# A spectral and token-mixing kernel: the order of PE and DVE written out, statistics block by block, products of a zeroed tile, moved tables and gate sums

## The chip, the core and the metric

The kernel runs on one core of a Trainium2 chip. A core has a matrix engine (PE) that multiplies a 128x128 stationary operand into a moving one and accumulates in PSUM, a vector engine (DVE), an activation engine (ACT), a general engine (POOL), and a queue engine (SP) that here only starts DMAs. Each runs its own list of instructions in order and waits on semaphores for the others. The metric is the device time of one execution in microseconds, lower is better; the runs before the change have a median of 156.61 us.

## What is computed

x is 2048 rows of 512, in bf16. The result mixes two branches, row by row, with a gate.

```python
g = _sigmoid((x * gate_w).sum(-1, keepdims=True))
# a: spectral filter
X = jnp.fft.rfft2(x.astype(jnp.float32), axes=(-2, -1)) * (w_r + 1j * w_i)
a = jnp.fft.irfft2(X, s=(S, D), axes=(-2, -1)).astype(jnp.bfloat16)
# b: token-mixing MLP, over the 2048 rows
h = _layernorm(x)
u = _gelu(jnp.einsum("bsd,sf->bdf", h, w1) + b1)
b = (jnp.einsum("bdf,fs->bds", u, w2) + b2).transpose(0, 2, 1)
return g * a + (1 - g) * b
```

S is 2048, D is 512, and the hidden width F is 1792, that is 14 columns of 128.

## The kernel before

**The MLP branch** works on x in 16 blocks of 128 rows. For each block, DVE makes mean and variance (`moments`: bn_stats, bn_aggr, an addition; POOL then takes the power -1/2), and DVE or ACT writes the normalised block hn (`normal`). The first six hidden columns (FT1 = 6) are accumulated over all 16 blocks at once in six PSUM banks, u1, from the weights w1a: six products of 128x512 per block (L248). The other eight columns come later, 16 products each, from w1b (L492). ACT evicts each column through a gelu into gl (`gelu`, L334). Then every block of the output takes 14 products from w2t into a bank yb (L505), which ACT evicts into tbv with the factor omg = 1 - g and the bias ombb2 (L507).

**The spectral branch** is a two-dimensional FFT by factors. xt is x transposed by four DMAs; the folds (L328, L329) make xf, sums and differences of its halves. Step f1 multiplies xf with the table tf into xdt, 16 blocks of four 256-column products (L343), each copied out by ACT (L345). `fft16` does a 16-point FFT across blocks on DVE alone, in two stages (p, r, q, s and their combinations), into fu. Step f3 multiplies fu with the table tce, 16 times three products (L414 to L417), and ACT copies to xs. `weight` multiplies four xs at a time with the filter wri into y (L407 to L410); a small side path (wn, ws, wrev, ghc with the permutations pmA and pmB, products L379 and L381, then u0, q, gu) treats the lowest column. Step i1 goes back with tice (L462, L464) into vp, a second `fft16` gives zt, step ya multiplies with tg (L478), ACT scales it by the gate (eo), DVE adds the halves (ap), and ot = tbv + ap is stored.

**The tables** tf, tg, tce and tice are sines: DVE makes integer arguments (m1t, m4t, marg, marg3), masks them to a period, and ACT takes the sine. Sines and gelus need different ACT tables, hence the ACT_TABLE_LOAD instructions. **The gate** is prod = x * gate weights on DVE (L323), summed per block by ACT with an accumulator (L352) into glog.

**What sets the order.** Between `startup.__enter__()` and `startup.__exit__()` the order of DVE, ACT, POOL and SP is that of the code, except that PE is not in the list. A planner orders PE everywhere and all engines after the exit; it puts products of u2 and yb into PE's free places. SP starts x and w1a in four pairs, then two transposes, w1b[0], two transposes, the rest of w1b, and wri. [...] PSUM has six banks for u1, u2 and yb and two ("ab") for f1, f3, i1, ya and the small steps. Scratch tiles with one tag share one buffer: `ffr` holds marg3 and then r of the FFT.

```python
startup = tc.manual_schedule(engines={E.DVE, E.Activation, E.Pool, E.SP})
home = {"x": 0, "fa": 0, "xs": 0, "ia": 0, "hn": 1, "vp": 1, "zt": 1, "xt": 2, "xdt": 2, "fu": 2, "ap": 2,
        "marg": 5, "xf": 3, "ea": 6, "y": 3, "wri": 4, "gl": 5, "prod": 6, "tbv": 6}
marg3 = tmp.tile([P, 2, NE, P], I16, tag="ffr", name="marg3")
```

`home` names the memory plane of each large tile; tiles in one plane follow each other in time.

Of the kernel before, what the change touches and what calls it, by code (L numbers as in the profile page):

```python
# [23 lines left out]
FT1 = 6  # L24
PI_IN = 3.1415925
# [80 lines left out]
def kernel(  # L106
# [24 lines left out]
    home = {"x": 0, "fa": 0, "xs": 0, "ia": 0, "hn": 1, "vp": 1, "zt": 1, "xt": 2, "xdt": 2, "fu": 2, "ap": 2,  # L131
            "marg": 5, "xf": 3, "ea": 6, "y": 3, "wri": 4, "gl": 5, "prod": 6, "tbv": 6}
# [11 lines left out]
    startup = tc.manual_schedule(engines={E.DVE, E.Activation, E.Pool, E.SP})  # L144
    startup.__enter__()

# [4 lines left out]
    for b0, b1 in ((0, 2), (2, 6), (6, 11), (11, 16)):  # L151
        w = wts.tile([P, b1 - b0, FT1 * P], BF16, tag="wt", name="w1a")
        nc.sync.dma_start(out=x[:, b0:b1], in_=xv[:, b0:b1])  # L153
# [4 lines left out]
    nc.gpsimd.dma_start(out=bias_rows[0:NFT], in_=B_b1.rearrange("(ft f) -> ft f", f=P))
    nc.gpsimd.dma_start(out=bias_rows[NFT:NFT + NB], in_=B_b2.rearrange("(b a) -> b a", a=P))
# [55 lines left out]
    nc.vector.tensor_copy(m1[:, :, 0], fix[:])  # L215
# [11 lines left out]
    def moments(b0, b1):  # L227
        bs = slice(b0, b1)
        for b in range(b0, b1):
            nc.vector.bn_stats(out=stats[:, b, :], in_=x[:, b, :])  # L230
        for b in range(b0, b1):
            nc.vector.bn_aggr(out=mv[:, b, :], in_=stats[:, b, :])
        nc.vector.tensor_scalar_add(rstd[:, bs], mv[:, bs, 1], 1e-5)
        nc.gpsimd.tensor_tensor(rstd[:, bs], rstd[:, bs], c_mhalf.to_broadcast([P, b1 - b0]), op=Alu.pow)
# [308 lines left out]
```

## Time and profile before

| | |
|---|---|
| runs | 156.5, 156.59, 156.63, 157.9 us; median 156.61 |
| profiled execution | 156.5 us, of which the span on the core is 154.7 us |
| granted PE clock, mean | 0.993 |
| instructions | 2013 |
| HBM | 19.02 MB read, 2.10 MB written |

The span runs from the first to the last instruction that the profiler recorded; the rest of an execution's time lies around it. In the timelines, a row has the start in us, the length, engine, line of the code, operation, the tile written and those read with partitions x elements and type, and the number of instructions merged; brackets hold the engine's idle time ahead of it and what ended that. In the groups, busy time and the mean in ns of one instruction stand behind the count. Lengths of neighbours overlap, so one instruction of a row of n costs a little less than its length.

### The profile page before, as it was taken

The numbers are of one execution on the slowest core, as the hardware profiler recorded it, in microseconds if no ns is written. First come the engines' busy times: TensorE is split into PE (matmuls) and PEld (weight loads), VectorE is DVE, ScalarE is ACT, GpSimd is POOL, SyncE is SP. The second block draws the span as 40 slices with busy tenths as digits, with TensorE's granted clock in tenths as the row PEclk, the third lists the DMA queues.
The fourth block names the chain that finished last, engine by engine and source line by source line (L and its number), as shares of the span: only waits on it lengthen the run. The fifth ranks groups of instructions, "written<-read, shape, count | busy, mean of one in ns | idle before, by whom it ended". The sixth has DMA issues, their size and how long they took to land.

```text
span 154.7 us, 2013 instructions
## 1 busy us (share of the span) xinstructions
PE 135.6 (88%) x697; PEld 68.0 (44%) x697; DVE 116.6 (75%) x279; ACT 94.7 (61%) x150; POOL 12.8 (8%) x37
## 2 busy tenths in 40 slices
PE   0078999969899999999959999999999969989990
PEld 0023444424456544444335565465444435655430
DVE  3988979969900399999994999507999999888111
ACT  3305564997199999999628897457223224978221
POOL 7117725000000000000000000000000000000000
PEclk9999999999999999999999999999999999999997
DMA  5999999999999304361800800250166100334210
GB/s 155 273 376 395 257 194 306 261 278 269 322 306 308 113 0 118 119 202 35 236 2 0 238 6 0 69 168 4 46 192 197 41 0 0 135 108 143 91 36 34
DMA packets 41816, 23.33 MB, mean 151 GB/s; under 512 B 9008, under 2 KB 41776, under 8 KB 41808
## 3 DMA queue, kind: packets, MB, share of 16 engines
q1 hardware_dynamic: 41696, 23.08, 52.6%
q0 software_dynamic: 112, 0.14, 0.3%
q8 instruction: 5, 0.08, 0.2%
q14 instruction: 3, 0.02, 0.1%
HBM read 19.02 MB, written 2.10 MB: 137 GB/s over the span
## 4 chain that ended last, share of the span: by engine, by line
DVE 46%; PE 21%; SPq 17%; ACT 7%; DMA 6%; issue 2%; DVEq 0%; ACTq 0%
SPq L172 10%; PE yb L505 9%; PE f L343 5%; DMA xt<-in_A_x_dram 4%; SPq L153 3%; DVE ta L407 3%; DVE prod L323 3%; DVE tb L408 3%; SPq L154 3%; ACT tice L204 2%; DMA out_dram<-ot 2%; DVE y L409 2%; PE ya L478 2%; DVE pb L39 2%; DVE ra L40 1%
## 5 line engine op out<-in xcount | busy, mean ns | idle before, releaser
L505 PE MATMUL yb<-gl,w2t 128*128 128x512 bf16 x224 | 53.6, 379 | 0.0
L505 PEld LDWEIGHTS <-w2t 128*128 128x128 bf16 x224 | 21.9, 98 | 21.5 <-issue 0.2
L492 PE MATMUL u<-hn,w1b 128*128 128x512 bf16 x128 | 29.3, 379 | 1.2 <-ACT gl L334 1.2
L507 ACT ACTIVATE tbv<-yb,ombb,omg 128x512 bf16<-128x512 f32 x16 | 12.4, 778 | 23.8 <-PE yb L505 22.4
L248 PE MATMUL u<-hn,w1a 128*128 128x512 bf16 x96 | 24.3, 419 | 1.5 <-DVE hn L245 1.5
L492 PEld LDWEIGHTS <-w1b 128*128 128x128 bf16 x128 | 12.5, 98 | 15.1 <-issue 1.5
L248 PEld LDWEIGHTS <-w1a 128*128 128x128 bf16 x96 | 10.1, 106 | 15.3 <-issue 6.1
L242 ACT ACTIVATE hn<-x,nmr,rstd 128x512 bf16<-128x512 bf16 x13 | 9.6, 802 | 9.8 <-DVE nmr L239 7.6
L481 ACT ACTIVATE eo<-ya,gs 128x512 bf16<-128x512 f32 x16 | 10.4, 687 | 4.9 <-DVE ap L484 2.7
L345 ACT CAST xdt<-f 128x512 bf16<-128x512 f32 x16 | 10.6, 735 | 4.0 <-DVE xf L329 3.5
L511 DVE TENSOR_TENSOR ot<-tbv,ap 128x512 bf16<-128x512 bf16 x16 | 6.7, 421 | 8.1 <-ACT tbv L507 7.5
L418 ACT CAST xs<-f 128x512 bf16<-128x512 f32 x16 | 9.1, 588 | 4.1 <-PE f L417 3.8
L478 PE MATMUL ya<-tg,zt 128*128 128x256 bf16 x64 | 9.3, 272 | 1.9 <-DVE zt L98 1.2
L466 ACT CAST vp<-i 128x512 bf16<-128x512 f32 x16 | 8.8, 587 | 2.8 <-PE i L464 2.6
L230 DVE BATCH_NORM_STATS2 stats<-x 128x6 f32<-128x512 bf16 x16 | 10.1, 680 | 0.4 <-DMA x<-in_A_x_dram 0.4
L352 ACT ACTIVATE junk<-prod 128x512 bf16<-128x512 bf16 x16 | 10.0, 626 | 0.3
L343 PE MATMUL f<-tf,xf 128*128 128x256 bf16 x64 | 9.6, 271 | 0.7 <-DVE xf L328 0.6
L334 ACT ACTIVATE gl<-u,biases 128x512 bf16<-128x512 f32 x14 | 9.0, 686 | 0.8 <-PE u L492 0.8
L478 PEld LDWEIGHTS <-zt 128*128 128x128 bf16 x64 | 6.1, 97 | 5.9 <-issue 1.9
L343 PEld LDWEIGHTS <-xf 128*128 128x128 bf16 x64 | 6.0, 96 | 5.5 <-issue 3.2
L462 PE MATMUL i<-tice,y 128*128 128x256 bf16 x32 | 7.8, 272 | 0.1
L39 DVE TENSOR_TENSOR pa<-xdt 128x2048 bf16<-128x2048 bf16 x1 | 1.2, 1225 | 8.9 <-ACT xdt L345 8.9
(178 smaller groups left out, 182.8 us busy)
## 6 DMA issues: line engine op xcount, KB each, us to landing
w2t<-in_B_w_dram SPq DMA_DIRECT2D x8, 896.0 KB, 5.1
w1b<-in_B_w_dram SPq DMA_DIRECT2D x4, 1024.0 KB, 8.9
out_dram<-ot SPq DMA_DIRECT2D x16, 128.0 KB, 1.7
w1a<-in_B_w_dram SPq DMA_DIRECT2D x2, 960.0 KB, 10.9
x<-in_A_x_dram SPq DMA_DIRECT2D x2, 640.0 KB, 10.6
wri<-in_A_w_r_dram SPq DMA_DIRECT2D x1, 1028.0 KB, 9.6
wri<-in_A_w_i_dram SPq DMA_DIRECT2D x1, 1028.0 KB, 10.1
w1a<-in_B_w_dram SPq DMA_DIRECT2D x1, 768.0 KB, 8.0
```

The lines of the kernel that those rows point to most:

```text
L172: nc.sync.dma_start(out=xt[:, dt], in_=xr[:, dt], transpose=True)
L230: nc.vector.bn_stats(out=stats[:, b, :], in_=x[:, b, :])
L242: nc.scalar.activation(hn[:, b, :], x[:, b, :], ActF.Identity, bias=nmr[:, b:b + 1], scale=rstd[:, b:b + 1])
L248: nc.tensor.matmul(u1[ft][:], lhsT=w1a[b][:, ft * P:(ft + 1) * P], rhs=hn[:, b, :], start=(b == 0), stop=(b == NB - 1))
L343: nc.tensor.matmul(bank[:, par * L:(par + 1) * L], lhsT=xf[:, par, kt, b * P:(b + 1) * P], rhs=tf[:, kt, par], start=(kt == 0), stop=(kt = ...
L345: nc.scalar.copy(xdt[:, b].rearrange("p c (i t) -> p t c i", t=2), bank[:].rearrange("p (t c i) -> p t c i", t=2, c=2))
L352: nc.scalar.activation(junk[:], prod[:, b], ActF.Copy, accum_out=glog[:, b:b + 1])
L478: nc.tensor.matmul(bank[:, par * L:(par + 1) * L], lhsT=zt[:, b, comp, par, :], rhs=tg[:, par, comp, :], start=(comp == 0), stop=(comp == 1))
L481: nc.scalar.activation(eo[:], bank[:].rearrange("p (t d) -> p t d", t=2), ActF.Copy, scale=gs[:, b:b + 1])
L492: nc.tensor.matmul(u[:], lhsT=w[:, b, k * P:(k + 1) * P], rhs=hn[:, b, :], start=(b == 0), stop=(b == NB - 1))
L505: nc.tensor.matmul(yb[:], lhsT=w[:, ft, k * P:(k + 1) * P], rhs=gl[:, ft, :], start=(ft == 0), stop=(ft == NFT - 1))
L507: nc.scalar.activation(tbv[:, b, :], yb[:], ActF.Identity, bias=ombb2[:, b:b + 1], scale=omg[:, b:b + 1])
```

## The change

It writes the order of PE too, up to the forward FFT, and that of DVE up to the last ap, and regroups the work:

- **Zero products.** PE starts with 12 products of a zeroed tile, into a bank that nobody reads.
- **Loads.** x and w1a come in eleven DMAs instead of eight, the first of a single block. On POOL, dcol and lrow come ahead of the two bias DMAs. The product that transposes the biases moves from PE's first place to behind block 9.
- **Statistics** go block by block, three stages interleaved (bn_stats of b, the rest of b-1, normalisation of b-2).
- **Gate.** Blocks 6 to 15 are multiplied and summed by one DVE instruction each; for 0 to 5 DVE multiplies in place and ACT sums. prod goes.
- **Folds** are done per pair of transposes, `fold(0)` and `fold(1)`, with six of the gate sums between.
- **Tables.** Arguments of tf and tg are 16-bit. tg, tce and tice are made behind the folds on DVE and behind f1 on ACT; marg, marg3 and ea share the plane idx, and fa lies in plane 3. The load of the gelu table is drawn ahead by a dummy gelu, `pre`.
- **PE order.** u1, hidden columns 6 and 7, f1 with column 8 threaded through it, columns 9 to 13, and the products of output blocks 0 and 1 (`yb_early`); from f3 on the planner fills in the other yb products.
- **Behind the FFT.** The sign and scale fixes of the tables, omg, gs, ombb2 and wn, ws follow the whole FFT on DVE; the rest of the side path (`packed_weights`) stands behind the second `weight`.

```diff
-    startup = tc.manual_schedule(engines={E.DVE, E.Activation, E.Pool, E.SP})
+    startup = tc.manual_schedule(engines={E.DVE, E.Activation, E.Pool, E.SP, E.PE})
+    zero = tmp.tile([P, D], BF16, tag="tws", name="zero")
+    nc.vector.memset(zero[:], 0.0)
+    warm = a_bank("warm")
+    for _ in range(WARM):
+        nc.tensor.matmul(warm[:], lhsT=zero[:, 0:P], rhs=zero[:], start=True, stop=True)
...
-    for b0, b1 in ((0, 2), (2, 6), (6, 11), (11, 16)):
-        w = wts.tile([P, b1 - b0, FT1 * P], BF16, tag="wt", name="w1a")
-        nc.sync.dma_start(out=x[:, b0:b1], in_=xv[:, b0:b1])
-        nc.sync.dma_start(out=w[:], in_=w1v[:, b0:b1, 0:FT1 * P])
...
+    for kind, b0, b1 in (("x", 0, 1), ("x", 1, 4), ("w", 0, 2), ("x", 4, 6), ("w", 2, 4), ("x", 6, 8), ("w", 4, 6), ("x", 8, 12), ("w", 6, 11), ("x", 12, 16), ("w", 11, 16)):
+        if kind == "x":
+            nc.sync.dma_start(out=x[:, b0:b1], in_=xv[:, b0:b1])
+        else:
+            w, g0 = wgroup[b0]
+            nc.sync.dma_start(out=w[:, b0 - g0:b1 - g0], in_=w1v[:, b0:b1, 0:FT1 * P])
...
-    m1t = tmp.tile([P, 2, 2, 2 * P], I32, tag="ffp", name="m1t")
+    m1t = tmp.tile([P, 2, 2, 2 * P], U16, tag="ffp", name="m1t")
...
+    def moments(b):
+        nc.vector.bn_aggr(out=mv[:, b, :], in_=stats[:, b, :])
+        nc.vector.tensor_scalar_add(rstd[:, b:b + 1], mv[:, b, 1:2], 1e-5)
+        nc.gpsimd.tensor_tensor(rstd[:, b:b + 1], rstd[:, b:b + 1], c_mhalf, op=Alu.pow)
...
+    sums(0)
+    moments(0)
+    for b in range(1, NB + 2):
+        if b < NB:
+            sums(b)
+        if b <= 3:
+            moments(b)
+            normal(b - 1)
+        elif b == 4:
+            normal_act(3)
+        elif b == 5:
+            moments(4)
+        else:
+            if b - 1 < NB:
+                moments(b - 1)
+            normal_act(b - 2)
...
+    pre = small.tile([P, 1], F32, name="pre")
+    nc.scalar.activation(pre[:], c_mhalf, ActF.Gelu_apprx_tanh)
+
+    def gate_sum(b0, b1):
         for b in range(b0, b1):
+            nc.vector.scalar_tensor_tensor(x[:, b], x[:, b], 1.0, gwb[:], op0=Alu.mult, op1=Alu.mult,
+                                           accum_out=glog[:, b:b + 1])
...
+    def fold(k):
+        nc.vector.tensor_add(xf[:, 0, k], xt[:, k], xt[:, k + 2])
+        nc.vector.tensor_sub(xf[:, 1, k], xt[:, k], xt[:, k + 2])
+
+    gate_sum(6, 10)
+    for b0 in (0, 3):
+        nc.vector.tensor_mul(x[:, b0:b0 + 3], x[:, b0:b0 + 3], gwb[:, None, :].to_broadcast([P, 3, D]))
+    fold(0)
...
+    gate_sum(10, NB)
+    fold(1)
...
+    for ft in (FT1, FT1 + 1):
+        u = mm_bank("u2")
+        for b in range(NB):
+            hidden(ft, u, b)
+        gelu(ft, u)
+    u = mm_bank("u2")
+    for b in range(NB):
...
+        if b >= 6:
+            hidden(FT1 + 2, u, b - 6)
+    for b in range(NB - 6, NB):
+        hidden(FT1 + 2, u, b)
+    gelu(FT1 + 2, u)
...
+    for ft in range(FT1 + 3, NFT):
+        u = mm_bank("u2")
+        for b in range(NB):
+            hidden(ft, u, b)
+        gelu(ft, u)
...
+    yb_early = [mm_bank("yb"), mm_bank("yb")]
+    for k in range(2):
+        for ft in range(NFT):
+            nc.tensor.matmul(yb_early[k][:], lhsT=early[:, ft, k * P:(k + 1) * P], rhs=gl[:, ft, :],
+                             start=(ft == 0), stop=(ft == NFT - 1))
...
+    nc.vector.tensor_scalar_mul(tce[:, 2], tce[:, 0], -1.0)
+    nc.vector.tensor_scalar_mul(tg[0:1, 0, :, :], tg[0:1, 0, :, :], 0.5)
+    nc.vector.tensor_scalar_mul(tice[:, :, 2], tice[:, :, 0], -1.0)
...
+    ombb2 = small.tile([P, NB], F32, name="ombb2")
+    nc.vector.tensor_mul(ombb2[:], omg[:], b2f)
...
+        if e == 7:
+            packed_weights()
...
+    def evict(b, yb):
+        nc.scalar.activation(tbv[:, b, :], yb[:], ActF.Identity, bias=ombb2[:, b:b + 1],
+                             scale=omg[:, b:b + 1])
+
+    for b in range(2):
+        evict(b, yb_early[b])
+    for c2 in range(1, NB // 2):
```

`normal(b)` and `normal_act(b)` do what `normal` did for one block on DVE or ACT and issue the block's six products; `sums(b)` is its bn_stats; `hidden(ft, u, b)` is one product of a later hidden column; `early` is w2t's first 256 columns.

The order of DVE around the start of the forward FFT. Before (L39 to L42 are p, q, r, s of the first stage, L54 to L59 parts of its output):

```order
L39 TENSOR_TENSOR pa<-xdt 128x2048
L41 TENSOR_TENSOR qa<-xdt 128x2048
L42 TENSOR_TENSOR sa<-xdt 128x2048
L54 TENSOR_TENSOR fa<-pa,qa 128x2048
L55 TENSOR_TENSOR fa<-pa,qa 128x1024
L56 TENSOR_TENSOR fa<-pa,qa 128x512
L58 TENSOR_TENSOR fa<-pa,qa 128x256
L59 TENSOR_TENSOR fa<-qa,pa 128x256
L349 TENSOR_SCALAR tice<-tice 128x16x128
L40 TENSOR_TENSOR ra<-xdt 128x2048
```

The same place after the change (idx holds the arguments of tce and tice):

```order
L380 TENSOR_TENSOR idx<-idx,m_374 128x2048
L381 TENSOR_SCALAR idx<-idx 128x2048
L215 TENSOR_SCALAR idx<-idx 128x4096
L391 TENSOR_SCALAR pmB<-spj 128x128
L392 TENSOR_SCALAR pmA<-spj 128x128
L393 TENSOR_SCALAR pmA_610<-spj 128x128
L394 TENSOR_TENSOR pmA<-pmA,pmA_610 128x128
L41 TENSOR_TENSOR pa<-xdt 128x2048
L42 TENSOR_TENSOR ra<-xdt 128x2048
L43 TENSOR_TENSOR qa<-xdt 128x2048
```

The table arguments and permutations have moved to right ahead of pa, and ra has moved from behind the tice fix to second place.

The order of ACT where the f3 copies (xs) begin. Before (junk, glog are the gate sums, tbv the eviction of an output block):

```order
L334 ACTIVATE gl<-u_1166,biases 128x512
L352 ACTIVATE junk,glog<-prod 128x512 x5
L334 ACTIVATE gl<-u_1184,biases 128x512
L354 ACTIVATE g<-glog 128x16
L507 ACTIVATE tbv<-yb,ombb_530,omg 128x512
L418 CAST xs<-f_626 128x512
L418 CAST xs<-f_631 128x512
```

After:

```order
L218 ACTIVATE tice<-idx,consts 128x2x16x128
L330 ACT_TABLE_LOAD
L330 ACTIVATE gl<-u_615,biases 128x512
L330 ACTIVATE gl<-u_633,biases 128x512
L330 ACTIVATE gl<-u_651,biases 128x512
L330 ACTIVATE gl<-u_669,biases 128x512
L330 ACTIVATE gl<-u_687,biases 128x512
L547 ACTIVATE tbv<-yb,ombb_810,omg 128x512 x2
L473 CAST xs<-f_820 128x512
L473 CAST xs<-f_825 128x512
```

The gate sums are gone from this place, the tice sine and its two table changes stand ahead of five gelus, and two evictions instead of one stand ahead of xs. Rows of the changed kernel carry its own line numbers.

260 lines of the change are left out of this document (114 added, 146 removed).

## The prediction

> **What bounds the kernel now.** I read the page's engine totals and its chain first, then busy time by stretch, then each engine's timeline at the stage borders.
>
> ```profile
> PE 135.6 (88%) x697; PEld 68.0 (44%) x697; DVE 116.6 (75%) x279; ACT 94.7 (61%) x150; POOL 12.8 (8%) x37
> DVE 46%; PE 21%; SPq 17%; ACT 7%; DMA 6%; issue 2%; DVEq 0%; ACTq 0%
> 12.00:16.20 4.20, 4.19 (x11) 1.45 (x11) 3.74 (x14) 2.22 (x3) 3.22 (x11) 1.00 1.07 394
> 16.20:33.60 17.40, 17.40 (x81) 7.82 (x80) 14.90 (x46) 13.03 (x14) 5.25 (x12) 1.00 1.12 249
> ```
>
> PE is the busiest engine, but the chain that ended last is nearly half DVE. In the stretches (length, then busy us and starts of PE, PEld, DVE, ACT and POOL, granted clock, DMA share, GB/s) 11 products start in 4.20 us, one per 0.4; after 16.2 it is one per 0.215, though the clock column reads 1.00 in both. I use 0.2155 us for a 512-column product (below: 40 in 8.80, the last of which lasts 0.38).
>
> ```profile
> 5.08 0.69 DVE L230 BATCH_NORM_STATS2 stats<-x 128x6 f32<-128x512 bf16 x1
> 26.01 0.18 DVE L302 COPY biases<-bias_t 128x30 f32<-128x30 f32 x1
> ...
> 33.39 4.63 DVE L323 TENSOR_TENSOR prod<-x,gwb 128x2048 bf16<-128x2048 bf16 x4
> 41.34 1.22 DVE L329 TENSOR_TENSOR xf<-xt 128x2048 bf16<-128x2048 bf16 x1
> 51.43 1.23 DVE L39 TENSOR_TENSOR pa<-xdt 128x2048 bf16<-128x2048 bf16 x1 [8.87 <-ACT xdt L345]
> 59.90 1.22 DVE L40 TENSOR_TENSOR ra<-xdt 128x2048 bf16<-128x2048 bf16 x1
> 78.78 1.22 DVE L100 TENSOR_TENSOR fu<-pb,qb 128x2048 bf16<-128x2048 bf16 x1
> 83.26 1.23 DVE L407 TENSOR_TENSOR ta<-xs,wri 128x2048 bf16<-128x2048 bf16 x1 [2.03 <-ACT xs L418]
> 98.24 0.68 DVE L410 TENSOR_TENSOR y<-tb,ta 128x1024 bf16<-128x1024 bf16 x1
> 105.56 1.23 DVE L39 TENSOR_TENSOR pa<-vp 128x2048 bf16<-128x2048 bf16 x1 [4.37 <-ACT vp L466]
> 129.06 1.22 DVE L100 TENSOR_TENSOR zt<-pb,qb 128x2048 bf16<-128x2048 bf16 x1
> ```
>
> This is DVE's timeline (start, length, work; in brackets the idle time ahead and its releaser). DVE does the statistics, the tables, prod and the folds until 42.6, idles 8.87 us, and runs the forward FFT from 51.4 to 80.0, 28.6 us. The inverse FFT, with nothing between, takes 105.56 to 130.3, 24.7 us.
>
> ```profile
> 42.64 2.75 ACT L345 CAST xdt<-f 128x512 bf16<-128x512 f32 x4 [3.50 <-DVE xf L329]
> 45.81 8.42 ACT L345 CAST xdt<-f 128x512 bf16<-128x512 f32 x12
> 55.54 3.71 ACT L204 ACTIVATE tice<-marg,consts 128x4096 bf16<-128x4096 int16 x1
> 59.68 0.19 ACT L352 ACTIVATION_READ_ACCUMULATOR junk<-prod 128x1 f32 x1
> 76.84 0.78 ACT L507 ACTIVATE tbv<-yb,ombb,omg 128x512 bf16<-128x512 f32 x1 [1.39 <-DVE ombb L360]
> 82.64 1.86 ACT L418 CAST xs<-f 128x512 bf16<-128x512 f32 x3 [0.19 <-PE f L417]
> ```
>
> On ACT the copies out of f1 wait for the folds and then run at 0.70 each (12 in 8.42). In the FFT ra comes only at 59.9: it takes the buffer of marg3, which the tice sine reads until 59.25.
>
> ```profile
> 24.81 8.80 PE L248 MATMUL u<-hn,w1a 128*128 128x512 bf16 x40
> 106.01 19.59 PE L505 MATMUL yb<-gl,w2t 128*128 128x512 bf16 x90
> 126.79 1.05 PE L478 MATMUL ya<-tg,zt 128*128 128x256 bf16 x8 [1.19 <-DVE zt L98]
> 140.84 9.66 PE L505 MATMUL yb<-gl,w2t 128*128 128x512 bf16 x44
> ```
>
> PE has spare yb products until 125.6, waits 1.19 us for the inverse FFT, and has 44 left when ya is done. So DVE's chain and PE's work meet within 1.2 us at 126.8, and a gain must shorten both.
>
> **The change, part by part.** The sum follows DVE; PE is checked beside it.
>
> *Start: loads, warm products, 16-bit tables.*
>
> ```profile
> 1.26 0.67 POOL L158 DMA_DIRECT2D bias_rows<-in_B_b_dram  x1 [0.81 <-POOLq L527]
> 2.55 0.16 POOL L183 IOTA dcol<- 128x2 f32 x1
> 4.47 0.69 DVE L201 TENSOR_SCALAR m1t<-m1t 128x1024 int32<-128x1024 int32 x1
> 1.76 0.46 SPq L153 DMA_DIRECT2D x<-in_A_x_dram  x1
> w1a<-in_B_w_dram SPq DMA_DIRECT2D x1, 384.0 KB, 3.2
> x<-in_A_x_dram SPq DMA_DIRECT2D x1, 512.0 KB, 6.5
> w1b<-in_B_w_dram SPq DMA_DIRECT2D x4, 1024.0 KB, 8.9
> ```
>
> dcol, on which the tables wait, moves ahead of POOL's two bias DMAs, 2.55 to 1.26. The mask of 1024 int32 takes 0.69, as long as 2048 int16 (below), so about 0.2 goes there: first statistics at 5.08 - 1.5 = 3.6. hn[0] then has the statistics of block 1 ahead of it, 2.3 in all: 5.9. w1a[0:2] is third in SP's queue, issued at 1.76: it lands between 5.0 (384 KB took 3.2 as the second) and 8.3 (the third took 6.5). I take 6.5, the middle, as PE's first product. The twelve warm products are through by then (from 1.3, at the cold pace of 0.42, until 6.4). They and the finer loads pull PE forward: 96 products from 6.5 end at 27.2 and two hidden columns (6.9) at 34.1. w1b[0] goes out ahead of the third transpose at 21.58 (below); at 8.9 it would land by 30.5, which moves 34.1 to 37.4 at worst. PE stands at 33.6 now when u1 ends, but what it gains counts only if DVE has the folds ready.
>
> *Statistics block by block.*
>
> ```profile
> L230 DVE BATCH_NORM_STATS2 stats<-x 128x6 f32<-128x512 bf16 x16 | 10.1, 680 | 0.4 <-DMA x<-in_A_x_dram 0.4
> 6.25 0.59 POOL L234 TENSOR_TENSOR rstd<-rstd,consts 128x1 f32<-128x1 f32 x1 [2.35 <-DVE rstd L233]
> ```
>
> Per block DVE needs 0.63 (10.1/16) and three small dependent instructions, together 0.4: 1.0 us. Bounds are 0.8 (the small ones packed) and 1.3 (a wait for a POOL power of 0.59 in each round). Blocks 1 to 3 add a normalisation, about 0.36. With 16 rounds, those, and 1.3 for the last two rounds and the bias copy, DVE is through at 3.6 + 16.0 + 1.1 + 1.3 = 22.0, against 26.2 now; bounds 18.8 and 26.8. PE's 6 x 0.2155 = 1.29 per block hides this pace. What left DVE here (tg, marg and marg3 tables) comes back behind the folds.
>
> *Gate sums and folds.* No row shows a two-source DVE instruction with an accumulator. Below it stands a quarter of a prod instruction, 0.3 (prod: 1.16 each); above, a statistics instruction (also 512 wide) plus ACT's accumulator read, 0.68 + 0.19 = 0.87. I take 0.75, nearer the row that also reduces; ten cost 7.5 (3.0 to 8.7). [...] Two products of 1536 take 1.75, four folds 4.55 (1.14 each), m0 and ae 0.55: fold 1 ends at 22.0 + 14.35 = 36.4. It also needs the last transpose, which the chain of waits shows:
>
> ```profile
> 21.58 5.26 SPq L172
> 26.88 6.04 DMA xt<-in_A_x_dram
> ```
>
> It landed at 32.9, behind the same bytes as after the change; with fold 1 behind it that gives 35.2. So DVE sets 36.4, PE (34.1) waits 2 us, and ACT, with six gelus, six sums of 0.75 and two gelus from about 26.5, is there at 36. The warm products and the loads are worth nothing past this point, unless DVE is faster than I think.
>
> *f1 and the tables.* With four products of 256 columns ahead (0.6) the first copy starts at 37.0; 16 at 0.70 end at 48.2, and the twelfth, which pa and ra need, at 45.4. The tables for tg, tce and tice now stand between fold 1 and pa on DVE (the DVE rows shown with the change).
>
> ```profile
> 17.13 1.39 DVE L258 TENSOR_SCALAR marg<-m,ae 128x128 int16<-128x128 int16 x8
> 26.20 0.69 DVE L307 TENSOR_SCALAR marg<-marg 128x2048 int16<-128x2048 int16 x1
> 30.05 1.23 DVE L201 TENSOR_SCALAR marg<-marg 128x4096 int16<-128x4096 int16 x1
> ```
>
> They cost 2 x 1.39, 5.1 for the five instructions from 26.20 to 31.28, about 1.5 for m4t in 16 bits and 0.8 for pmA and pmB: 10.2, so pa starts at 46.6. The former idle time pays for all but 1.2 us of it; if f1 came earlier this cover would be gone and the tables would hold pa. The sines lie on ACT behind the copies, and marg3 has a buffer of its own, so ra follows pa: 24.7 for the FFT gives 71.3, against 80.0.
>
> *Behind the FFT.* DVE then writes the three table fixes, omg, gs and ombb2 (1.8 by the widths above): 73.1. ACT has two evictions ahead of xs (the ACT rows with the change), which need ombb2 and take 2 x 0.73: 74.6. Four xs copies at 0.6 follow: the first weighting starts at 77.0, against 83.26. PE arrives with the early products at 72.2 (f1 and column 8 about 49, five columns 17.2, 28 products 6.0) and waits here too. The weighting stage took 98.92 - 83.26 = 15.7; packed_weights, now inside it, adds 1.3: 94.0. The inverse FFT starts 6.6 later and ya 21.2 after that: 121.8. PE beside it: its spare run starts 0.45 behind the FFT's start, at 101.1, and 91 products take 19.6: 120.7. DVE is late by 1.1, as now.
>
> *End.* From ya to the end took 154.7 - 126.79 = 27.9. 28 products stand behind ya instead of 44, so 16 x 0.2155 = 3.45 goes: 121.8 + 24.45 = 146.25. The execution reported 156.5 for a span of 154.7, 1.8 more: **148.0**. The median of the runs is 156.61, 0.1 above that execution; I leave it out.
>
> **Rivals.**
>
> 1. *PE binds.* The gate sums cost 0.3, so the transpose sets f1 at 35.2 (1.2 earlier), and the evictions do not delay xs (2.3 less). Then zt is ready at 118.3, but PE comes at 119.5 and sets the end: 145.7. [...] Against: both must hold.
> 2. *DVE slower.* The loop at 1.3 per block (+4.8) or the sums at 0.87 (+1.2) go straight to the end: 149 to 154. For: from 22 to 71 DVE has no slack, and sixteen powers on POOL stand where six stood.
> 3. *The warm-up does nothing.* If w1a lands at 8.3, PE has stood idle for 2 us since the warm products. If the pace is cold again, ten products cost 0.2 more: u1 ends at 8.3 + 20.7 + 2.1 = 31.1 and the hidden columns at 38.0, 1.6 behind DVE: 149.6. For: now, the cold pace lasts until 16.2. Against: the 1.19 us pause at 126.8 left the pace at 0.2155 (44 in 9.66). [...]
> 4. *Slower than before.* SP's eleven cut loads move at half the rate, and the transposes behind them come late, so f1 does. To lose the 8.6 gained and 1.6 more, f1 must start at 46.6 instead of 36.4, so xt must land past 43, and x and w1 would need some 10 us more. Against: the rows have the same length in memory as now, and moved at 394 GB/s in the stretch above. Time 158 or more from there.
> 5. *Nothing gained.* The loss behind the FFT is not 3.6 us (evictions and packed_weights) but 8, because weightings, evictions and xs wait for each other through two PSUM banks: 156 at most. Against: the four weightings took 15.7 now, 3.9 per round, under the same banks.
>
> **How the numbers follow.** Forecast 0.55 (its own range 146.5 to 150), PE binds 0.14, DVE slower 0.16, no warm-up 0.06, slower 0.05, nothing gained 0.04. The range leaves out the last two and the far ends of rivals 1 and 2: 145.5 to 152.8. About 1% is what a measurement of this kernel can tell from no change: faster 0.91 (the first four), same 0.04, slower 0.05.
>
> **What would show it.** First statistics near 3.6; PE at 0.2155 per product from about 6.5; bias copy near 22; gate sums of 0.75; f1 copies from 37; pa near 46.6 with ra right behind it and no idle of 8 us on DVE; weighting near 77; ya near 121.8 with 28 products behind it. A fold that waits for xt, DVE rounds released by POOL, a weighting that waits on ACT for long, or PE idle for over 3 us ahead of f1 would prove it wrong.

## The result, and the profile after

The changed kernel takes 146.96 us (median of 11 runs, 146.65 to 147.8) against 156.67 (16 runs beside it, 155.71 to 158.08): a ratio of 0.939, with a 95% interval of 0.936 to 0.942. The forecast was 148.0, within 145.5 to 152.8. The profiled execution reported 147.1 for a span of 145.0; that of before had 154.7.

The page of the changed kernel, engine totals and the chain that ended last:

```profile
PE 135.9 (94%) x709; PEld 69.1 (48%) x709; DVE 121.7 (84%) x317; ACT 89.2 (61%) x131; POOL 15.8 (11%) x47
PE 36%; DVE 33%; SPq 18%; ACT 5%; DMA 3%; issue 2%; DVEq 0%; ACTq 0%
```

PE is busy as long as before, in a span 9.7 us shorter; DVE has 5 us more. DVE's share of the chain fell from 46% to 33%.

DVE's timeline of the changed kernel, at the marks that the prediction used (start, length, work, idle ahead with its releaser):

```profile
2.86 0.68 DVE L242 BATCH_NORM_STATS2 stats<-x 128x6 f32<-128x512 bf16 x1
4.73 0.69 DVE L242 BATCH_NORM_STATS2 stats<-x 128x6 f32<-128x512 bf16 x1 [0.79 <-DMA x<-in_A_x_dram]
...
21.02 0.18 DVE L292 COPY biases<-bias_t 128x30 f32<-128x30 f32 x1
...
30.59 0.69 DVE L301 SCALAR_TENSOR_TENSOR x<-x,gwb 128x512 bf16<-128x512 bf16 x1
...
31.20 0.69 DVE L301 SCALAR_TENSOR_TENSOR x<-x,gwb 128x512 bf16<-128x512 bf16 x1
...
32.04 1.23 DVE L307 TENSOR_TENSOR xf<-xt 128x2048 bf16<-128x2048 bf16 x1
33.18 1.22 DVE L308 TENSOR_TENSOR xf<-xt 128x2048 bf16<-128x2048 bf16 x1
...
44.14 1.22 DVE L41 TENSOR_TENSOR pa<-xdt 128x2048 bf16<-128x2048 bf16 x1
45.28 1.22 DVE L42 TENSOR_TENSOR ra<-xdt 128x2048 bf16<-128x2048 bf16 x1
46.97 1.23 DVE L43 TENSOR_TENSOR qa<-xdt 128x2048 bf16<-128x2048 bf16 x1 [0.48 <-ACT xdt L354]
...
68.39 1.22 DVE L102 TENSOR_TENSOR fu<-pb,qb 128x2048 bf16<-128x2048 bf16 x1
...
75.11 1.23 DVE L462 TENSOR_TENSOR ta<-xs,wri 128x2048 bf16<-128x2048 bf16 x1 [3.38 <-ACT xs L473]
...
99.45 1.23 DVE L41 TENSOR_TENSOR pa<-vp 128x2048 bf16<-128x2048 bf16 x1 [4.37 <-ACT vp L523]
```

The wait of 8.87 us ahead of pa is gone, since the tables stand there now, and ra follows pa at once. The forward FFT ends at 69.6, 10.4 earlier, the first weighting starts 8.2 earlier, and the inverse FFT 6.1.

PE's timeline of the changed kernel:

```profile
1.20 5.14 PE L153 MATMUL warm<-zero 128*128 128x512 bf16 x12 [1.20 <-DVE zero L150]
6.20 5.62 PE L251 MATMUL u<-hn,w1a 128*128 128x512 bf16 x24
...
27.93 7.07 PE L334 MATMUL u<-hn,w1b 128*128 128x512 bf16 x32
34.84 1.04 PE L352 MATMUL f<-tf,xf 128*128 128x256 bf16 x8
...
73.37 0.38 PE L469 MATMUL f<-fu,tce 128*128 128x512 bf16 x1 [1.07 <-ACT xs L473]
...
120.81 1.05 PE L535 MATMUL ya<-tg,zt 128*128 128x256 bf16 x8 [1.10 <-DVE zt L100]
...
134.21 6.64 PE L559 MATMUL yb<-gl,w2t 128*128 128x512 bf16 x30
```

The warm products go at 0.43 each; the 24 behind them stand 0.23 apart at first, and 32 hidden products take 7.07, 0.216 each. u1 ends at 27.9 instead of 33.6. ya starts 6.0 earlier, with 30 products behind it instead of 44: 14 x 0.2155 = 3.0 more. The rest of the 9.7 lies between ya's first row and those products.

ACT's timeline of the changed kernel around f1 and ahead of f3:

```profile
27.06 3.58 ACT L330 ACTIVATE gl<-u,biases 128x512 bf16<-128x512 f32 x6 [3.40 <-PE u L251]
...
34.74 0.24 ACT L412 ACTIVATE g<-glog 128x16 f32<-128x16 f32 x1
35.04 0.69 ACT L330 ACTIVATE gl<-u,biases 128x512 bf16<-128x512 f32 x1
35.63 11.31 ACT L354 CAST xdt<-f 128x512 bf16<-128x512 f32 x16
...
71.39 1.45 ACT L547 ACTIVATE tbv<-yb,ombb,omg 128x512 bf16<-128x512 f32 x2 [5.72 <-DVE ombb L430]
```

Here the run departs from the forecast, which had DVE last: the folds end at 34.40, but the first copy out of f1 comes only at 35.63. The gelu of the second hidden column stands ahead of it; it starts at 35.04, when PE ends that column (27.93 + 7.07 = 35.00) and ACT has g behind it (34.98). So three chains arrive within 0.6 us: DVE's folds, PE's column, ACT's queue. A fourth lies close ahead of them. This is its row in the chain that ended last:

```profile
26.88 5.07 DMA xt<-in_A_x_dram
```

The last transpose landed at 31.95. DVE was done with the gate sums at about 31.81 (the last two start 0.61 apart), so fold(1) waited some 0.2 us for xt.

### The profile page after: what moved, and what is told of

Its sections match the earlier page's. It is cut to its first block, busy times and chain, and to the rows that moved or that the text cites. A ratio compares the mean times of both kernels' runs of the same rounds, so it can differ in the third digit from the quotient of the medians.

```text
span 145.0 us, 2078 instructions
## 1 busy us (share of the span) xinstructions
PE 135.9 (94%) x709; PEld 69.1 (48%) x709; DVE 121.7 (84%) x317; ACT 89.2 (61%) x131; POOL 15.8 (11%) x47
## 4 chain that ended last, share of the span: by engine, by line
PE 36%; DVE 33%; SPq 18%; ACT 5%; DMA 3%; issue 2%; DVEq 0%; ACTq 0%
PE yb L559 15%; SPq L183 12%; PE ya L535 6%; PE f L352 4%; DMA xt<-in_A_x_dram 3%; SPq L170 3%; PE i L519 3%; SPq L167 3%; PE f L469 3%; ACT xdt L354 2%; PE i L521 2%; DVE pb L41 2%; DVE qa L43 2%; DVE sa L44 2%; DVE rb L42 2%
## 5 line engine op out<-in xcount | busy, mean ns | idle before, releaser
L559 PE MATMUL yb<-gl,w2t 128*128 128x512 bf16 x196 | 48.2, 379 | 0.0
L559 PEld LDWEIGHTS <-w2t 128*128 128x128 bf16 x196 | 19.2, 99 | 17.6
L251 PE MATMUL u<-hn,w1a 128*128 128x512 bf16 x96 | 21.4, 379 | 0.4 <-ACT hn L262 0.4
L251 PEld LDWEIGHTS <-w1a 128*128 128x128 bf16 x96 | 9.3, 97 | 12.2 <-issue 1.3
L262 ACT ACTIVATE hn<-x,nmr,rstd 128x512 bf16<-128x512 bf16 x13 | 10.4, 812 | 7.4 <-DVE nmr L260 6.5
L242 DVE BATCH_NORM_STATS2 stats<-x 128x6 f32<-128x512 bf16 x16 | 10.9, 685 | 0.8 <-DMA x<-in_A_x_dram 0.8
L564 DVE TENSOR_TENSOR ot<-tbv,ap 128x512 bf16<-128x512 bf16 x16 | 6.6, 419 | 4.7 <-ACT tbv L547 4.4
L247 POOL TENSOR_TENSOR rstd<-rstd,consts 128x1 f32<-128x1 f32 x16 | 9.1, 570 | 7.6 <-DVE rstd L246 4.5
L462 DVE TENSOR_TENSOR ta<-xs,wri 128x2048 bf16<-128x2048 bf16 x4 | 4.9, 1222 | 3.5 <-ACT xs L473 3.4
```

Source lines behind the costliest of these rows:

```text
L251: nc.tensor.matmul(u1[ft][:], lhsT=w1a[b][:, ft * P:(ft + 1) * P], rhs=hn[:, b, :], start=(b == 0), stop=(b == NB - 1))
L262: nc.scalar.activation(hn[:, b, :], x[:, b, :], ActF.Identity, bias=nmr[:, b:b + 1], scale=rstd[:, b:b + 1])
L559: nc.tensor.matmul(yb[:], lhsT=w[:, ft, k * P:(k + 1) * P], rhs=gl[:, ft, :], start=(ft == 0), stop=(ft == NFT - 1))
```

## Experiments

Two theories stood after the result. *On record:* DVE sets the start of f1 and nearly all that follows, so the warm products and finer loads buy nothing behind f1. *From the trace:* PE, through u1 and two columns, sets f1, and is so full behind it that any delay of PE's reaches the end. The kernels below are the changed one with one edit each, except before_marg3, which edits the kernel before. Their medians are of 4 runs each (before_marg3: 10; stt_probe: 1), and the kernel before ran beside them at 156.55 to 156.96.

| kernel | time | span | u1 ends | first f1 copy | ya starts | yb products behind ya |
|---|---|---|---|---|---|---|
| changed | 146.96 | 145.0 | 27.93 | 35.63 | 120.81 | 30 |
| no_warm_2 | 148.64 | 146.0 | 28.89 | 36.59 | 121.75 | 29 |
| old_loads | 148.41 | 146.5 | 29.34 | 37.03 | 122.22 | 29 |
| old_start | 148.51 | 146.4 | 29.33 | 37.03 | 122.21 | 29 |
| dve_plus3 | 148.44 | 146.3 | 27.46 | 36.62 | 122.05 | 29 |
| f1_early | 146.53 | 144.7 | 28.18 | 34.99 | 120.46 | 30 |
| xs_first | 146.05 | 144.1 | 27.98 | 35.67 | 120.12 | 28 |
| no_early | 147.76 | 146.1 | 28.11 | 35.80 | 119.06 | 42 |
| f1_early_no_yb | 146.97 | 146.2 | 28.57 | 36.09 | 119.62 | 40 |
| marg3_ffr | 154.44 | 152.3 | 27.57 | 35.26 | 131.31 | 0 |
| before | 156.67 | 154.7 | 33.6 | 42.64 | 126.79 | 44 |
| before_marg3 | 155.51 | 153.5 | 32.6 | 42.08 | 122.83 | 56 |

The last column counts the last run of products; a product or two can be missing from a trace (no_warm_2 has 31 of the 32 hidden products ahead of f1). Where PE's order is written, "u1 ends" is the start of its next product; in the two kernels at the bottom it is the end of its last. The marks are those of one execution each. The start alone moves them: in the executions of kernels with the same start, u1 ends between 27.46 (dve_plus3) and 28.57 (f1_early_no_yb). What stays is the distance: in the seven rows whose work between u1 and f1 is that of the changed kernel (changed, no_warm_2, old_loads, old_start, xs_first, no_early, marg3_ffr), the first f1 copy comes 7.69 or 7.70 us behind u1's end. In f1_early it is 6.81, in dve_plus3 9.16.

**Without the warm products.**

```
-    zero = tmp.tile([P, D], BF16, tag="tws", name="zero")
-    nc.vector.memset(zero[:], 0.0)
-    warm = a_bank("warm")
-    for _ in range(WARM):
-        nc.tensor.matmul(warm[:], lhsT=zero[:, 0:P], rhs=zero[:], start=True, stop=True)
```

> The changed kernel without the twelve zero products, nothing else. Theory A (the pace of PE depends on how long it has been busy, and only part of it is covered): the first ten or so products of hn start at 0.42 us instead of 0.2155, so u1 ends 2.0 us later (near 30.0) and the first copy out of f1 comes at 36.8 instead of 35.63; every later mark moves by 1.2, time near 148.2. Theory B (the one on record: PE stands ahead of DVE, the folds hide it): f1 hardly moves, 147.2 or less. Theory C (PE's work is the bound from here on, nothing hides it): the full 2.0, near 149.0.

Measured: 147.88, 148.08 and 147.85 us, and a profiled execution of 282.6, told of under the hardware below. The same kernel was run a second time:

> The kernel without the twelve zero products once more, since its profiled execution before was one in which PE kept 0.45 us per product for the whole span (280.5 us), so that no profile of an ordinary execution was at hand. Theory A: ten or so products at 0.42 from about 6.2, u1 ends near 30, first copy out of f1 at 36.6, time 148.0. Theory B (the loss of 1.0 us lies elsewhere, in the loads or in ACT): the products of hn run at 0.2155 from the start and f1 is late for another reason. If the slow execution belongs to a kernel without warm products, it comes again in some of these runs.

Measured: 148.64 us (148.07 to 149.45), and no execution like that one. The seven ordinary executions of this kernel (median 148.08) all lie above the slowest of the changed kernel's, 147.8. PE's first row in no_warm_2, and the busy time by stretch (length, then PE, PEld, DVE, ACT and POOL with the number of instructions at work in it, the granted clock, DMA):

```profile
6.14 6.07 PE L245 MATMUL u<-hn,w1a 128*128 128x512 bf16 x19 [6.14 <-DVE hn L249]
...
8.00:10.00 2.00, 2.00 (x7) 0.69 (x5) 1.93 (x8) 0.56 (x1) 0.65 (x1) 1.00 1.03 361
10.00:12.00 2.00, 2.00 (x11) 0.88 (x9) 1.90 (x10) 1.00 (x2) 1.10 (x2) 1.00 1.07 400
```

Seven products are at work in the first of these stretches, eleven in the second, and the clock column reads 1.00 in both. The row of 19 has 18 distances in 6.07 - 0.38 = 5.69 us: eight or nine at 0.43 and the rest at 0.2155, 1.8 us more than 18 at 0.2155. u1 ends 0.96 later, the first f1 copy 0.96 later (theory A: 36.6), and ya 0.94. So f1 is where theory A put it, by another way. It had u1 near 30.0 and part of the loss covered at f1. In fact half of the 1.8 is gone by u1's end, since in the changed kernel PE needs 21.7 us from 6.20 to 27.93 for products worth 96 x 0.2155 = 20.7, and 0.35 of the rest is its wait for hn at 12.18; behind u1 nothing covered any of it. Their starts do not make the difference: the statistics of block 2 begin at 6.00 in no_warm_2 and at 6.06 in the changed kernel. Theory B and the sentence on record fall. In this trace the change of pace came 3.4 to 3.9 us behind the first product (eight or nine distances of 0.43). It is not as regular in others: the twelve zero products take 5.14 us in the changed kernel, 0.43 each to the end, but 4.15 in xs_first.

**Loads as before.** x and w1a in turn, four groups each:

```
-    for kind, b0, b1 in (("x", 0, 1), ("x", 1, 4), ("w", 0, 2), ("x", 4, 6), ("w", 2, 4), ("x", 6, 8), ("w", 4, 6), ("x", 8, 12), ("w", 6, 11), ("x", 12, 16), ("w", 11, 16)):
+    for b0, b1 in ((0, 2), (2, 6), (6, 11), (11, 16)):
+        w, g0 = wgroup[b0]
+        nc.sync.dma_start(out=x[:, b0:b1], in_=xv[:, b0:b1])
+        nc.sync.dma_start(out=w[:], in_=w1v[:, b0:b1, 0:FT1 * P])
```

> The changed kernel with the loads of x and w1a cut as before: x and w1a in turn, in four groups of 2, 4, 5 and 5 blocks. Theory A (x[2:6] lands third in the queue near 8 us, where the statistics now want block 2 at 6): DVE waits about 2 us there, u1 ends 2 us later, f1 takes 1.2 of it, 148.2. Theory B (the finer loads buy nothing past the folds, as the record has it): 147.2 or less. Theory C (fewer and larger loads leave SP earlier and the transposes land earlier): up to 0.5 faster, 146.5.

Measured: 148.41 us. DVE's statistics of block 2 and PE's hidden columns in old_loads:

```profile
7.46 0.69 DVE L240 BATCH_NORM_STATS2 stats<-x 128x6 f32<-128x512 bf16 x1 [1.62 <-DMA x<-in_A_x_dram]
...
29.34 7.07 PE L332 MATMUL u<-hn,w1b 128*128 128x512 bf16 x32
```

DVE waited 1.62 for block 2. u1, f1 and ya are all 1.4 later, the span 1.5. Theory A had the place right; of the 2 us that it expected at u1 1.4 came, and f1 took all of it, not 1.2 of 2.

**The start as before.** Bias DMAs ahead of dcol on POOL, m1t in int32, lrow in float32:

```
+    nc.gpsimd.dma_start(out=bias_rows[0:NFT], in_=B_b1.rearrange("(ft f) -> ft f", f=P))
+    nc.gpsimd.dma_start(out=bias_rows[NFT:NFT + NB], in_=B_b2.rearrange("(b a) -> b a", a=P))
     dcol = iota([P, 2], "dcol", [[P, 2]], 1)
-    m1t = tmp.tile([P, 2, 2, 2 * P], U16, tag="ffp", name="m1t")
+    m1t = tmp.tile([P, 2, 2, 2 * P], I32, tag="ffp", name="m1t")
```

> The changed kernel with the start as before: POOL's two bias DMAs ahead of dcol, and the tables m1t and lrow in 32 bits. Theory on record (these two are worth 1.5 us at the first statistics, and DVE has no slack): first statistics near 4.4 instead of 2.86, every mark 1.5 later, 148.5. Theory from the trace (the statistics of block 1 wait 0.79 us for their load now, which such a delay fills, and f1 has some 0.6 of slack): u1 0.7 later, f1 0.1 later, 147.1.

Measured: 148.51 us. DVE and PE in old_start:

```profile
5.13 0.69 DVE L243 BATCH_NORM_STATS2 stats<-x 128x6 f32<-128x512 bf16 x1
...
29.33 7.07 PE L335 MATMUL u<-hn,w1b 128*128 128x512 bf16 x32
```

The first statistics came 2.27 later, not 1.5. The load wait of 0.79 took up part, as the theory from the trace had it, but its slack at f1 did not exist: 1.40 reached u1, f1 and ya. The time is the one that the record's theory gave, by another way: its 1.5 went through DVE, this 1.40 through PE.

**More DVE work ahead of fold(1).**

```
     gate_sum(10, NB)
+    for k in range(3):
+        nc.vector.scalar_tensor_tensor(spare[:], x[:, 15], 1.0, gwb[:], op0=Alu.mult, op1=Alu.mult,
+                                       accum_out=scrap[:, k:k + 1])
     fold(1)
```

> The changed kernel with three more gate-sum instructions ahead of fold(1), results unused: 3 x 0.61 = 1.83 us of DVE, of which 0.15 fills its wait for the last transpose. Theory on record (DVE has no slack from 22 to 71, an excess goes straight to the end): every mark behind fold(1) moves by 1.7, 148.7. Theory from the trace of the change (fold(1) ended 0.45 ahead of PE's first f1 product and about 0.6 ahead of what ACT could copy): the first copy out of f1 moves from 35.63 to 36.7, qa to 48.05, the end by 1.1: 148.1. Rival (PE is the bound and DVE has slack): under 0.3, 147.2.

Measured: 148.44 us, between the first two theories. DVE, PE and ACT in dve_plus3:

```profile
35.02 1.22 DVE L308 TENSOR_TENSOR xf<-xt 128x2048 bf16<-128x2048 bf16 x1
...
48.24 1.22 DVE L43 TENSOR_TENSOR qa<-xdt 128x2048 bf16<-128x2048 bf16 x1
...
36.30 0.72 PE L357 MATMUL f<-tf,xf 128*128 128x256 bf16 x5 [0.74 <-DVE xf L308]
...
36.62 11.32 ACT L359 CAST xdt<-f 128x512 bf16<-128x512 f32 x16 [1.37 <-PE f L357]
```

The fold moved by 1.84 and f1 by 0.99, near the 36.7 of the theory from the trace. Now PE waits for the fold, which it did not in the changed kernel. DVE had about 0.8 us of slack towards f1, but less in its own list: the tables behind fold(1) are 1.8 later too, and qa, which has lost its wait of 0.48, starts at 48.24 instead of 46.97. That 1.27 reached the end: ya is 1.24 later, and the span grew by 1.3. The theory had 1.1, through f1.

**f1 freed from PE's column and ACT's queue.**

```
-    for b in range(6):
-        nc.scalar.activation(x[:, b], x[:, b], ActF.Copy, accum_out=glog[:, b:b + 1])
...
+    for b in range(NB - 6):
+        hidden(FT1 + 1, v, b)
...
         if b >= 6:
             hidden(FT1 + 2, u, b - 6)
+        else:
+            hidden(FT1 + 1, v, NB - 6 + b)
```

> The changed kernel with f1 freed from the second hidden column and from ACT's queue: six of that column's products go between the first six f1 blocks, its gelu behind the copies, the six gate sums of ACT to the end of its written order. Theory A (f1 waits for PE's second column and its gelu; the folds are 0.6 ahead): first copy at 34.9 instead of 35.63, PE's gaps among the f1 blocks filled, qa at 46.4 without a wait, 146.4. Theory B (f1 is paced by the folds or by ACT's copies alone): first copy and end unchanged, 146.9.

Measured: 146.53 us (146.1 to 146.75). That is 0.4 less than the changed kernel in the median, but the two sets of runs overlap. PE, ACT and DVE in f1_early:

```profile
34.67 0.28 PE L352 MATMUL f<-tf,xf 128*128 128x256 bf16 x1 [0.40 <-DVE xf L308]
...
34.99 11.33 ACT L354 CAST xdt<-f 128x512 bf16<-128x512 f32 x16 [2.48 <-PE f L352]
...
46.62 1.22 DVE L43 TENSOR_TENSOR qa<-xdt 128x2048 bf16<-128x2048 bf16 x1
...
73.02 0.38 PE L474 MATMUL f<-fu,tce 128*128 128x512 bf16 x1 [1.34 <-ACT xs L478]
```

The first copy comes 0.64 earlier, though u1 and the folds are 0.2 later in this execution: theory A holds, the folds were not what f1 waited for in the changed kernel. But ya moves by 0.35 only. DVE's tables now fill the time to qa, which starts at 46.62 without a wait, 0.35 earlier, and PE waits 1.34 ahead of f3 instead of 1.07. So DVE stands only half a microsecond behind PE here, as dve_plus3 shows from the other side, and part of the gain became another wait. Whether PE's column or ACT's sums held f1 is not told apart, since both went.

**marg3 back in the FFT's buffer.**

```
-    marg, marg3 = idx[:, 0:2], idx[:, 2:4]
+    marg = idx[:, 0:2]
+    marg3t = tmp.tile([P, 2, NE, P], I16, tag="ffr", name="marg3")
```

> The changed kernel with marg3 back in FFT buffer r, nothing else. Theory A (the buffer is what held ra): ra waits for the sine of tice, which ends at 58.27, and starts 13.0 later than 45.28; qa's wait of 0.48 goes, so the forward FFT ends near 82.0 and the weighting starts near 87.6, ya near 133. PE fills the gap with the yb products that now lie behind ya, so the end moves by less than the 12.5: about 6 for the 28 products, 152 to 154. Theory B (DVE's chain alone counts): 159.5. Theory C (the planner hides it): 147.

Measured: 154.44 us. DVE and PE in marg3_ffr:

```profile
57.92 1.22 DVE L42 TENSOR_TENSOR ra<-xdt 128x2048 bf16<-128x2048 bf16 x1 [12.93 <-ACT tice L218]
...
131.31 1.05 PE L537 MATMUL ya<-tg,zt 128*128 128x256 bf16 x8 [1.10 <-DVE zt L100]
...
136.06 1.18 PE L537 MATMUL ya<-tg,zt 128*128 128x256 bf16 x8 [0.67 <-ACT eo L540]
```

Theory A, a little past its 152 to 154: ra waits 12.93 us, ya comes 10.5 later, the span grows by 7.3. PE used the gap for all 30 products, and then ya itself waits for ACT.

**The same buffer in the kernel before.** To make room, two other things change there: ACT's gate sums write back into prod instead of junk, and the output sums lie in a plane of their own instead of three buffers in turn.

```
-    marg3 = tmp.tile([P, 2, NE, P], I16, tag="ffr", name="marg3")
+    marg3 = small.tile([P, 2, NE, P], I16, name="marg3")
```

> The kernel before with marg3 in a buffer of its own instead of FFT buffer r; to make room the gate sums on ACT write back into prod and the output sums lie in the plane of y. Theory on record: ra follows pa at once and the forward FFT takes 24.7 instead of 28.6 us, so it ends near 76 and the first weighting comes near 79.5; but PE had only 1.19 us of waiting left at ya, so the end moves by about 1.2: 155.4. Rival (DVE's chain alone sets the end): the whole 3.9 arrives, 152.7. Rival (the buffer held nothing that mattered): 156.6.

Measured: 155.51 us against 156.96 beside it, a ratio of 0.992 (0.988 to 0.996). DVE and PE in before_marg3:

```profile
52.01 1.22 DVE L40 TENSOR_TENSOR ra<-xdt 128x2048 bf16<-128x2048 bf16 x1
...
122.83 1.05 PE L477 MATMUL ya<-tg,zt 128*128 128x256 bf16 x8 [1.19 <-DVE zt L98]
...
136.81 12.47 PE L504 MATMUL yb<-gl,w2t 128*128 128x512 bf16 x56
```

ra follows pa (50.87) at once, but the forward FFT does not take the 24.7 us of the theory: it runs from 50.87 to 78.43, 27.6, since omg, gs, ombb2, the permutations, ws and wrev stand in it. Most of them stand in it in the kernel before, too. So of the 3.9 between 28.6 and 24.7 the buffer accounts for about 1. The first weighting still comes at 79.31, where the theory had 79.5, because its wait of 2.03 for xs has shrunk to 0.19, and because f1 began 0.56 earlier in this execution.

ya starts 3.96 earlier and the end comes 1.45 earlier: 56 products now lie behind ya instead of 44, 12 x 0.2155 = 2.6. From PE's last product to the end both kernels take 4.2, so the changed output buffers have no part in it. In this the theory on record holds: DVE's gain alone arrives as more work left for PE.

**Evictions that need not wait for ombb2.** omg, gs and ombb2 go ahead of the forward FFT; the fixes of tg and tice behind the first weighting:

```
     written.__enter__()
+    omg = small.tile([P, NB], F32, name="omg")
...
+        if e == 3:
+            nc.vector.tensor_scalar_mul(tg[0:1, 0, :, :], tg[0:1, 0, :, :], 0.5)
+            nc.vector.tensor_scalar_mul(tice[:, :, 2], tice[:, :, 0], -1.0)
```

> The changed kernel with omg, gs and ombb2 ahead of the forward FFT (into DVE's 0.48 wait for xdt) and with the fixes of tg and tice behind the first weighting. Theory A (the evictions in front of xs waited for ombb2, and PE and DVE both waited for that): evictions end near 71.7, first xs there instead of 72.73, first weighting 74.1 instead of 75.11, ya 1.0 earlier, time near 146.0. Theory B (PE is the bound and its 1.10 wait ahead of ya only grows shorter): PE loses its 1.07 wait in f3, and ya's remains, also about 1.0. Theory C (the stage behind gives it back, at l0q or in the fixes put behind the first weighting): 147.0.

Measured: 146.05 us, the fastest kernel here: its runs (145.81 to 146.25) all lie under those of the changed kernel, though the intervals of the two ratios overlap (0.924 to 0.938). ACT and DVE in xs_first:

```profile
71.08 0.78 ACT L547 ACTIVATE tbv<-yb,ombb,omg 128x512 bf16<-128x512 f32 x1 [2.24 <-PE yb L408]
71.76 1.06 ACT L470 CAST xs<-f 128x512 bf16<-128x512 f32 x2
...
74.12 1.23 DVE L459 TENSOR_TENSOR ta<-xs,wri 128x2048 bf16<-128x2048 bf16 x1 [3.43 <-ACT xs L470]
```

The second eviction now follows PE, the first xs comes 0.97 earlier, PE's wait of 1.07 in f3 is gone, and the span is 0.9 shorter. PE's 1.1 ahead of ya stayed.

**Without the early yb columns.**

```
-    yb_early = [mm_bank("yb"), mm_bank("yb")]
-    for k in range(2):
-        for ft in range(NFT):
-            nc.tensor.matmul(yb_early[k][:], lhsT=early[:, ft, k * P:(k + 1) * P], rhs=gl[:, ft, :],
-                             start=(ft == 0), stop=(ft == NFT - 1))
```

> The changed kernel without the early yb columns: all sixteen are left to the planner, which evicts none ahead of the first xs. Theory A (the evictions ahead of xs cost both PE and DVE a wait, and the early columns gain nothing that spare work would not): first xs near 70.8 instead of 72.73, first weighting near 73.9 instead of 75.11, PE's wait of 1.07 in f3 gone, 145.8. Theory B (PE has nothing ready while DVE ends the FFT, since the planner puts too little there): PE waits ahead of f3 and the time is 147 or more.

Measured: 147.76 us. PE in no_early:

```profile
66.41 0.59 PE L462 MATMUL f<-fu,tce 128*128 128x512 bf16 x2 [1.27 <-DVE fu L100]
...
119.06 1.05 PE L528 MATMUL ya<-tg,zt 128*128 128x256 bf16 x8 [1.11 <-DVE zt L100]
...
132.46 9.44 PE L550 MATMUL yb<-gl,w2t 128*128 128x512 bf16 x42
```

Both theories saw a part. DVE is 1.5 earlier at the first weighting (73.64) and 1.75 at ya, yet the time is 0.8 longer: the planner puts f3's first products on PE ahead of its spare ones, and PE waits 1.27 for fu. Its wait of 1.07 in f3 is gone, as theory A had it, but short waits of up to 0.23 (for tce, vp and eo) have come; PE is idle 1.0 us longer in all, and 42 products are left behind ya. A faster DVE chain with an idle PE loses.

**Both of the last ideas for f1 and f3.**

> Both edits of the two kernels before at once. Theory A (they act at different places and add up): 145.3. Theory B (PE's work is the bound by then, and only its waits count): the larger of the two gains alone, 145.8.

Measured: 146.97 us (146.72 to 148.3), no gain on the changed kernel. The edits are those of f1_early and no_early. The profiled execution is the 148.3, in which fold(1) came 1.3 later than in the changed kernel, so its marks decide little; PE's wait for fu, 1.52, is there as well.

**What the gate sum's price comes from.** Ahead of fold(1), results unused, two each of the form without accumulator, a plain product, and a one-source form with accumulator:

```
+        nc.vector.scalar_tensor_tensor(spare[:], x[:, 15], 1.0, gwb[:], op0=Alu.mult, op1=Alu.mult)
+        nc.vector.tensor_mul(spare[:], x[:, 15], gwb[:])
+        nc.vector.tensor_scalar(spare[:], x[:, 15], 1.0, 0.0, op0=Alu.mult, op1=Alu.add, accum_out=scrap[:])
```

> The changed kernel with six instructions of 512 columns ahead of fold(1), results unused: two of the gate sum's form without the accumulator, two plain products, two one-source instructions with an accumulator. Theory A (the accumulator sets the price of the gate sum): the form without it is as cheap as a plain product, about 0.42 long and 0.33 apart, and the one-source form with it stands 0.6 apart. Theory B (the form itself is slow whatever it reads and writes): without the accumulator it stands 0.6 apart as well.

DVE in stt_probe, from the last gate sum on:

```profile
30.70 0.69 DVE L301 SCALAR_TENSOR_TENSOR x<-x,gwb 128x512 bf16<-128x512 bf16 x1
...
31.44 1.42 DVE L328 SCALAR_TENSOR_TENSOR spare<-x,gwb 128x512 bf16<-128x512 bf16 x2
32.89 0.88 DVE L330 TENSOR_TENSOR spare<-x,gwb 128x512 bf16<-128x512 bf16 x2
33.80 0.69 DVE L332 TENSOR_SCALAR_CACHE_REDUCE spare<-x 128x512 bf16<-128x512 bf16 x1
```

Two of the form without accumulator take 1.42, two plain products 0.88, each pair into the same tile. So theory B: the form is as slow without the accumulator. The one-source form with one is as slow too (0.69). This is one run.

## Why the prediction was right, and where it was not

- **Start.** First statistics at 2.86, forecast 3.6; first hn product at 6.20 against 6.5. Right, and about 0.3 to 0.7 pessimistic. The counts in the prediction's first rows were read as starts; they are the products at work in the stretch. In the 4.20 us some ten start, 0.43 apart, not one per 0.4. Nothing in the sum hangs on it.
- **Statistics block by block.** 1.0 us per block was forecast; the bias copy ended at 21.20 against 22.0. No wait for POOL's power held it but two of 0.32 and 0.36 at the end.
- **Gate sums: the size was off.** 0.75 each was forecast; they stand 0.61 apart. Ten of them: 1.4 us. The reason was half right: the row that it was taken from (a statistics instruction, 0.68) fits, but the accumulator's read adds nothing, since it lies beside the next instruction (in the changed kernel the product behind the fourth gate sum starts at 23.57, as the read does, which is 0.08 long, and 0.62 behind that sum's start at 22.95). The prediction's lower bound, 0.3 from a quarter of a prod instruction, does not hold for this form: with both sources in bf16 it takes 0.69, where a plain product takes 0.42 (ot, L564) to 0.44 (stt_probe).
- **What sets f1: the step that failed.** The prediction had "DVE sets 36.4, PE (34.1) waits 2 us", and so "the warm products and the loads are worth nothing past this point". It allowed for this "unless DVE is faster than I think", and it was: the folds ended at 34.4, 2.0 early (0.8 from the statistics, 1.4 from the gate sums, 0.2 lost again to the transpose at 31.95). PE's column, at 35.0, was 0.9 late, and came 0.6 behind the folds with ACT's gelu. A fold that waits for xt, which the prediction named as a sign against itself, is there with some 0.2 us. no_warm_2, old_loads and old_start show what that step was worth: 0.96, 1.4 and 1.4 us of f1, each of which went to the end. That the total came out within 1.1 us is in part luck: two terms were off in opposite directions, DVE's by 2.0 and PE's by 0.9, and the later of the two moved f1 by 1.4 only.
- **marg3's own buffer.** Forecast: ra right behind pa, 24.7 for the FFT. Measured: 25.5 from pa to fu's end, of which 0.48 is qa's wait. The number is right; without the buffer the time is 154.44, since the tice sine now ends only at 58.3. But the buffer is not all that made the FFT shorter: in before_marg3, which has the buffer and still runs small instructions within the FFT, it took 27.6. The other part is that these and the table fixes now stand behind it.
- **Evictions and packed_weights behind the FFT.** First weighting at 75.11 against 77.0, then 17.4 us until y is done against 17.0. Right: f1's earlier start carries the difference.
- **End.** From ya to the end 24.2 against 24.45, with 30 products behind it. The 28 of the forecast stand without a working, so that they came so near is not shown to be more than luck. "A gain must shorten both" is shown by before_marg3 and no_early from the one side, by no_warm_2 and xs_first from the other.
- **Rivals.** *PE binds* (145.7) is nearest to what happened, though neither of its two conditions held: PE sets f1 and the end, with the gate sums at 0.61 and the evictions ahead of xs still costing 1.07, which xs_first takes away (146.05). *DVE slower* did not come. *The warm-up does nothing* fell by no_warm_2. For *slower*, xt would have had to land past 43; it landed at 31.95. For *nothing gained*, the loss behind the FFT would have had to be 8; it was 4.0, against 3.6 forecast: 2.3 more ahead of the first weighting and 1.7 more in the stage. (A loss of 8 would add 4.4 to the forecast, 152.4, so that rival's "156 at most" does not follow from its own number.)

In sum the span came out 1.25 below the 146.25 worked out. The marks were 1.4 early at f1, 1.7 at the end of the forward FFT and 1.9 at the first weighting; the weighting stage and l0q gave 0.9 of it back, so ya was 1.0 early, and the end after it took 0.25 less. The statistics block by block, the gate sums on DVE and the new place of the tables were not taken back one by one, so their shares of the gain are not shown.

## What to carry to other kernels

When one engine is busy for nine tenths of the span, count its waits, not the marks of the chain beside it: here 4 us gained on DVE alone gave 1.45, and 1 us of PE's start gave 1. Where several chains meet within a microsecond, price an edit on each of them, since a small error in one term (0.14 us on ten instructions) decides which of them sets the pace. And a wait that you take away can show up as the next one: look for it there (f1's 0.64 became 0.35 at qa and ya).

## What the runs showed of the hardware

One execution of the kernel without warm products took 282.6 us; seven others of it took 147.85 to 149.45. Its busy time between 100 and 200 us (columns as above):

```profile
100.00:200.00 100.00, 98.83 (x264) 40.62 (x267) 36.06 (x66) 26.91 (x44) 0.00 (x0) 1.00 0.16 46
```

PE ran at half pace to the end, though it was busy for 99 of 100 us; 24 hidden products took 11.49 there, 0.48 each, and the clock column reads 1.00. The other engines' instructions took as long as ever: DVE's 128x2048 product (ta) 1.223 us and ACT's gelu 0.690 in the mean, against 1.222 and 0.692 in the changed kernel. That the missing warm products caused it is not shown: none of the 11 executions of the changed kernel did this, but neither did any of the kernel before, which has none either.

The second thing is the price of the two-source form with bf16 sources, 0.61 to 0.73 us per 512 columns: 0.61 in the gate sums, where each writes to its own place, and 0.73 in dve_plus3, where all three write to the same (starts at 31.80, 32.53 and 33.27). That the shared place is the reason is not shown. The third is that the load of x[1:4] kept the statistics of block 1 waiting between 0.17 and 1.0 us in profiled executions of the same loads (dve_plus3 and f1_early), so marks of two kernels that differ by less than that at the start say little by themselves.
